# A small tile in front is widened by 128 bytes, and the tiles behind it lie elsewhere

## The chip, the cores and the metric

The kernel runs on one core of a Trainium2 chip. Its time is the device time in microseconds, the median of several runs. A profile of one execution shows what each engine did. The engines are TensorE (PE; its weight loads are listed apart, as PEld), VectorE (DVE), ScalarE (ACT), GpSimd (POOL) and SyncE (SP), which issues the DMAs here.

## What is computed

An attention with pooled keys and values, then a mixture of 8 experts with all experts weighted for each token, then a feed-forward layer with softplus. There are 2304 tokens of 512 numbers. Cut to what matters:

```
x = attention(q, k, v)                       # 4 x 8 heads, 576 queries, 72 pooled keys, width 64
P = balance(exp(x @ w_gate - max))           # 2304 x 8, rows and columns scaled 8 times
y = sum over e of P[:, e] * (relu(x @ w1[e]) @ w2[e])      # w1[e] 512 x 1024, w2[e] 1024 x 512
h = y @ w_in                                 # 512 x 2048
out = softplus(h) @ w_out                    # 2048 x 512
```

## The kernel before

Every matrix that enters one of the large products is held as two tiles, a rounded one (hi) and the rest (lo), and each product of two matrices is made of three matmuls: hi-hi, hi-lo and lo-hi. The function `three` (L439) writes them; all its matmuls have line L443 in the profile.

The work goes by units u of 512 hidden columns: 16 units for the 8 experts, 4 for the last layer (20 in all). In each unit the tokens go by 5 blocks, four of 512 and one of 256. For a block, `first_product` (L445) makes four tiles ph (f = 0 to 3) of 128 hidden columns by 512 tokens. The stationary operand (the weight that is loaded into TensorE) is a 128x128 slice of w1hi or w1lo, and the streamed operand is xhi or xlo, 512 columns at a time, 256 in the short block. ScalarE and VectorE turn ph into hhi and hlo (L469, L470); in the last four units the softplus takes eight operations and GpSimd writes hlo (L479 to L487). `second_product` (L490) then makes, for each 128 tokens of the block, a tile py of 128 tokens by 512: here a 128x128 slice of hhi or hlo is the stationary operand, the weight that is loaded, and w2hi or w2lo is streamed. There are 18 such tiles to a unit and 12 matmuls to a tile. The "second product's weight tiles" of this case are therefore hhi and hlo.

The order of the instructions is the order of the code: the first product of a block runs ahead by two tiles f (SKEW), then the second product of the block before follows. In the first unit the attention's steps stand between the products. In the units of the experts, the gate (`gate`, L317, tiles pg, stationary wg_r of 16 columns, streamed x) and the balancing are put between the products, and later a conversion of the last layer's weights.

Tiles get their place in memory by pools, one after the other from the left: const, xT (xhi, xlo), w (w1hi, w1lo, w2hi, w2lo), raw, sk, and behind them what is opened later (first the pools h0, ld, at and ld_x, then h, tmp and dec in the same place). The bytes for each of the 128 partitions, and where they lie:

```
start 16512; ident 512, ones 512, wg 128, wg_r 256   -> wg_r at 17664 = 34 x 512 + 256
xhi, xlo 36864 each                                  -> xhi at 17920 = 35 x 512, xlo at 54784 = 107 x 512
12 tiles w1hi .. w2lo, 2 raw tiles, 4096 each        -> w1hi at 91648 = 179 x 512, w2hi at 116224 = 227 x 512
prob 576, row 96 (72 and padding), col 64, big 32, lg 1152
pools h0 (later h): hhi, hlo 2048 each               -> the first at 150912 = 294 x 512 + 384
```

A slice for one matmul is 512 bytes further than the slice before it (128 numbers of 4 bytes), so all slices of hhi and hlo start 384 bytes past a multiple of 512, and all of w1hi, w1lo, w2hi, w2lo, xhi and xlo at one. (wg_r's four slices start 64 bytes apart.) Tiles in pools opened on the right side (acc0, acc1, ld_e, at_e) are placed from the other end.

Of the kernel before, what the change touches and what calls it, by code (L numbers as in the profile page):

```python
# [9 lines left out]
F32 = mybir.dt.float32  # L10
# [9 lines left out]
def attention_moe_softplus_kernel(  # L20
# [15 lines left out]
    E = w_gate.shape[1]  # L36
# [10 lines left out]
    P = 128  # L47
# [23 lines left out]
    kpool = ctx.enter_context(tc.tile_pool(name="sk", bufs=1))  # L71
# [12 lines left out]
    prob = kpool.tile([P, NT, E], F32, name="prob")  # L84
    row = kpool.tile([P, NT], F32, name="row")

    col = kpool.tile([P, 2 * E], F32, name="col")[:, :E]
    big = kpool.tile([P, 2], F32, name="big")
    lg = kpool.tile([P, NT, 2 * E], F32, name="lg")
    nc.scalar.preload_act_table_set("natural_log_exp_and_others")  # L90
# [526 lines left out]
```

## Time and profile before

| what | before |
|---|---|
| median of 3 runs | 2134.09 us (2132.28 to 2134.9) |
| profiled execution, its own time | 2131.61 us |
| its span, first to last instruction | 2129.8 us |
| mean granted TensorE clock | 0.997 |
| TensorE busy | 2108.9 us (99%) |
| VectorE, ScalarE, GpSimd busy | 975.7, 534.8, 409.4 us |

The span is what the profile's rows cover; the profiled execution's own time is 1.8 us more, and the runs of the table's first line lie a little higher still. A granted clock of 1.00 is the 2.4 GHz level of TensorE's two (1.2 and 2.4 GHz). "The chain that ended last" follows the work back from the last instruction to whatever released each step.

### The profile page before, as it was taken

The numbers are of one execution on the slowest core, as the hardware profiler recorded it, in microseconds if no ns is written. First come the engines' busy times: TensorE is split into PE (matmuls) and PEld (weight loads), VectorE is DVE, ScalarE is ACT, GpSimd is POOL, SyncE is SP. The second block draws the span as 40 slices with busy tenths as digits, with TensorE's granted clock in tenths as the row PEclk, the third lists the DMA queues.
The fourth block names the chain that finished last, engine by engine and source line by source line (L and its number), as shares of the span: only waits on it lengthen the run. The fifth ranks groups of instructions, "written<-read, shape, count | busy, mean of one in ns | idle before, by whom it ended". The sixth has DMA issues, their size and how long they took to land.

```text
span 2129.8 us, 24079 instructions
## 1 busy us (share of the span) xinstructions
PE 2108.9 (99%) x9893; PEld 1727.8 (81%) x9893; DVE 975.7 (46%) x1574; ACT 534.8 (25%) x946; POOL 409.4 (19%) x281
## 2 busy tenths in 40 slices
PE   7999999999999999999999999999999999999999
PEld 5777788888888888888888888888888878888887
DVE  7772344544334433444344344222222355667665
ACT  4443211111111111111111111111111246545443
POOL 5441101111110101111101111110101023333332
PEclk8999999999999999999999999999999999999999
DMA  6320101111111101111111111000100000000001
GB/s 167 100 72 12 38 11 55 40 45 50 50 36 49 60 25 60 40 45 50 59 40 45 40 60 35 25 30 10 30 10 30 11 30 11 30 11 30 11 35 54
DMA packets 66333, 87.54 MB, mean 41 GB/s; under 512 B 22448, under 2 KB 38832, under 8 KB 66224
## 3 DMA queue, kind: packets, MB, share of 16 engines
q1 hardware_dynamic: 66224, 86.01, 13.0%
q8 instruction: 77, 1.26, 0.2%
q14 instruction: 32, 0.26, 0.0%
HBM read 72.89 MB, written 13.11 MB: 40 GB/s over the span
## 4 chain that ended last, share of the span: by engine, by line
PE 94%; DVE 3%; ACT 1%; POOL 1%; issue 0%; DMA 0%; SPq 0%; POOLq 0%; ACTq 0%; DVEq 0%
PE py L443 46%; PE ph L443 44%; PE px L249 1%; PE s L209 1%; DVE cr L483 1%; PE pa L238 1%; POOL hlo L487 1%; PE pg L317 0%; PE pt L516 0%; DVE ln L485 0%; DMA qt<-in_q_dram 0%; PE pq L181 0%; ACT ex L480 0%; ACT ln L482 0%; ACT cr L481 0%
## 5 line engine op out<-in xcount | busy, mean ns | idle before, releaser
L443 PE MATMUL ph<-xhi,w1hi 128*128 128x512 f32 (+1 forms) x1600 | 591.7, 370 | 0.0
L443 PE MATMUL ph<-xhi,w1lo 128*128 128x512 f32 (+1 forms) x1600 | 589.4, 368 | 0.0
L443 PE MATMUL ph<-xlo,w1hi 128*128 128x512 f32 (+1 forms) x1600 | 589.1, 368 | 0.0
L443 PE MATMUL py<-w2hi,hhi 128*128 128x512 f32 x1440 | 571.4, 397 | 0.0
L443 PE MATMUL py<-w2hi,hlo 128*128 128x512 f32 x1440 | 569.0, 395 | 0.8 <-POOL hlo L487 0.2
L443 PE MATMUL py<-w2lo,hhi 128*128 128x512 f32 x1440 | 567.9, 394 | 0.0
L469 ACT ACTIVATE hhi<-ph 128x512 fp32r<-128x512 f32 (+1 forms) x320 | 177.9, 556 | 1191.1 <-PE ph L443 1149.2
L470 DVE SCALAR_TENSOR_TENSOR hlo<-ph,hhi 128x512 fp32r<-128x512 f32 (+1 forms) x320 | 203.8, 637 | 541.0 <-ACT hhi L469 540.9
L507 DVE SCALAR_TENSOR_TENSOR acc<-py,prob,acc 128x512 f32<-128x512 f32 x252 | 189.1, 751 | 386.9 <-PE py L443 386.4
L443 PEld LDWEIGHTS ph<-xhi,w1hi 128*128 128x128 f32 x1600 | 301.6, 189 | 55.5 <-issue 3.9
L443 PEld LDWEIGHTS ph<-xlo,w1hi 128*128 128x128 f32 x1600 | 301.6, 189 | 51.1 <-DVE xlo L252 0.6
L443 PEld LDWEIGHTS ph<-xhi,w1lo 128*128 128x128 f32 x1600 | 301.6, 188 | 50.6
L443 PEld LDWEIGHTS py<-w2hi,hlo 128*128 128x128 f32 x1440 | 271.1, 188 | 68.0 <-POOL hlo L487 4.7
L443 PEld LDWEIGHTS py<-w2hi,hhi 128*128 128x128 f32 x1440 | 271.3, 188 | 65.9 <-issue 5.0
L443 PEld LDWEIGHTS py<-w2lo,hhi 128*128 128x128 f32 x1440 | 271.5, 189 | 61.1
L121 POOL TENSOR_TENSOR w1lo<-w1raw,w1hi 128x1024 fp32r<-128x1024 f32 x40 | 98.0, 2450 | 457.1 <-ACT w1hi L120 457.1
L121 POOL TENSOR_TENSOR w2lo<-w2raw,w2hi 128x1024 fp32r<-128x1024 f32 x40 | 97.2, 2431 | 397.9 <-ACT w2hi L120 397.8
L487 POOL TENSOR_TENSOR hlo<-ln,hhi 128x512 fp32r<-128x512 f32 (+1 forms) x80 | 104.9, 1311 | 271.1 <-DVE hhi L486 223.7
L421 POOL TENSOR_TENSOR dt<-dt,da 128x512 f32<-128x512 f32 x32 | 41.4, 1295 | 493.6 <-issue 297.6
L483 DVE SCALAR_TENSOR_TENSOR cr<-cr,ex 128x512 f32<-128x512 f32 (+1 forms) x80 | 75.3, 942 | 112.2 <-ACT ln L482 112.1
L479 ACT ACTIVATE ex<-ph 128x512 f32<-128x512 f32 (+1 forms) x80 | 44.2, 553 | 135.3 <-PE ph L443 132.1
L502 DVE TENSOR_TENSOR acc<-py,acc 128x512 f32<-128x512 f32 x72 | 47.5, 686 | 53.6 <-PE py L443 53.6
(86 smaller groups left out, 1107.0 us busy)
## 6 DMA issues: line engine op xcount, KB each, us to landing
w1raw<-in_moe_w_dram SPq DMA_DIRECT2D x32, 512.0 KB, 3.3
w2raw<-in_moe_w_dram SPq DMA_DIRECT2D x32, 512.0 KB, 3.5
f<-in_moe_w_in_dram SPq DMA_DIRECT2D x16, 512.0 KB, 4.2
v<-dt SPq DMA_DIRECT2D x32, 256.0 KB, 2.1
f<-in_moe_w_out_dram SPq DMA_DIRECT2D x16, 512.0 KB, 3.6
kt<-in_k_dram SPq DMA_DIRECT2D x16, 288.0 KB
qt<-in_q_dram SPq DMA_DIRECT2D x32, 144.0 KB, 2.8
vt<-in_v_dram SPq DMA_DIRECT2D x16, 288.0 KB
```

Of the source, the lines that this page charges most:

```text
L121: nc.gpsimd.tensor_tensor(lo, raw, hi.bitcast(F32), op=ALU.subtract)
L209: nc.tensor.matmul(ps[:QP, j * 2 * SP:(j + 1) * 2 * SP], qT[:, j * QP:(j + 1) * QP], kbd[g % 2])
L238: nc.tensor.transpose(pa[:SP, j * QP:(j + 1) * QP], ex[:, 2 * j + h, :], ident[:QP, :QP])
L421: nc.gpsimd.tensor_tensor(t, t, a.bitcast(F32), op=ALU.add)
L443: nc.tensor.matmul(ps, a, b, start=first and i == 0, stop=last and i == 2)
L469: nc.scalar.activation(hh, ph[:, :n], AF.Relu)
L470: nc.vector.scalar_tensor_tensor(hl, ph[:, :n], 0.0, hh.bitcast(F32), op0=ALU.max, op1=ALU.subtract)
L479: nc.scalar.activation(e, ph[:, :n], AF.Abs)
L483: nc.vector.scalar_tensor_tensor(c, c, 1.0, e, op0=ALU.subtract, op1=ALU.subtract)
L487: nc.gpsimd.tensor_tensor(hl, l, hh.bitcast(F32), op=ALU.subtract)
L502: nc.vector.tensor_tensor(a, py, a, op=ALU.add)
L507: nc.vector.scalar_tensor_tensor(a, py, prob[:, t, e:e + 1], a, op0=ALU.mult, op1=ALU.add)
```

## The change

The tile col, 8 numbers of which are used, is given 48 numbers instead of 16. That is 192 bytes instead of 64 for each partition, and all that is placed behind it from the left moves up by 128 bytes: big, lg, the tiles of the attention's pools, hhi and hlo, and the temporary tiles of the later stages. The first hhi lies at 151040 = 295 x 512 then, and all slices of hhi and hlo start at a multiple of 512. The tiles in front of col, and those placed from the right, stay where they are. Each engine has the same instructions in the same order, with the same waits.

```
-    col = kpool.tile([P, 2 * E], F32, name="col")[:, :E]
+    col = kpool.tile([P, 6 * E], F32, name="col")[:, :E]
     big = kpool.tile([P, 2], F32, name="big")
     lg = kpool.tile([P, NT, 2 * E], F32, name="lg")
```

## Rows read from the trace of the kernel before

**Rows 1.** Busy time of each engine, share of the span and instructions.

```profile
PE 2108.9 (99%) x9893; PEld 1727.8 (81%) x9893; DVE 975.7 (46%) x1574; ACT 534.8 (25%) x946; POOL 409.4 (19%) x281
```

**Rows 2.** The chain that ended last, shares by engine and by line.

```profile
PE 94%; DVE 3%; ACT 1%; POOL 1%; issue 0%; DMA 0%; SPq 0%; POOLq 0%; ACTq 0%; DVEq 0%
PE py L443 46%; PE ph L443 44%; PE px L249 1%; PE s L209 1%; DVE cr L483 1%; PE pa L238 1%; POOL hlo L487 1%; PE pg L317 0%; PE pt L516 0%; DVE ln L485 0%; DMA qt<-in_q_dram 0%; PE pq L181 0%; ACT ex L480 0%; ACT ln L482 0%; ACT cr L481 0%
```

**Rows 3.** Pieces of that chain, 724 to 791 us: start, length, what, count.

```profile
724.84 10.90 PE ph L443 x48
735.74 11.16 PE py L443 x48
746.89 10.89 PE ph L443 x48
757.78 11.15 PE py L443 x48
...
779.83 11.16 PE py L443 x48
```

**Rows 4.** Two of its longest pieces in the whole span.

```profile
790.99 11.20 PE ph L443 x72
...
2109.26 16.75 PE py L443 x72
```

**Rows 5.** Busy time, granted clock and DMA in three of those pieces.

```profile
core 0: us, PE busy (x) PEld busy (x) DVE busy (x) ACT busy (x) POOL busy (x), PEclk, DMA share, GB/s
735.74:746.89 11.15, 11.15 (x49) 9.04 (x49) 2.94 (x4) 0.60 (x1) 3.47 (x2) 1.00 0.34 118
746.89:757.78 10.89, 10.89 (x50) 9.01 (x49) 4.19 (x7) 2.73 (x4) 1.07 (x1) 1.00 0.00 0
757.78:768.93 11.15, 11.15 (x50) 9.04 (x49) 5.60 (x9) 0.60 (x1) 2.12 (x2) 1.00 0.13 48
```

**Rows 6.** Timeline of TensorE around a gate: start, length, operation, count.

```profile
209.76 1.09 PE L317 MATMUL pg<-xhi,wg_r 128*16 128x512 f32 x4
210.69 1.09 PE L317 MATMUL pg<-xlo,wg_r 128*16 128x512 f32 x4
211.62 0.40 PE L443 MATMUL ph<-xhi,w1hi 128*128 128x512 f32 x1
```

**Rows 7.** Groups of matmuls and weight loads by form: busy us, mean ns.

```profile
L443 PE MATMUL py<-w2hi,hhi 128*128 128x512 f32 x1440 | 571.4, 397 | 0.0
L443 PE MATMUL py<-w2hi,hlo 128*128 128x512 f32 x1440 | 569.0, 395 | 0.8 <-POOL hlo L487 0.2
L443 PE MATMUL py<-w2lo,hhi 128*128 128x512 f32 x1440 | 567.9, 394 | 0.0
...
L443 PEld LDWEIGHTS ph<-xhi,w1hi 128*128 128x128 f32 x1600 | 301.6, 189 | 55.5 <-issue 3.9 <-PE px L249 0.4 <-DVE mx L216 0.4
...
L443 PEld LDWEIGHTS py<-w2hi,hhi 128*128 128x128 f32 x1440 | 271.3, 188 | 65.9 <-issue 5.0 <-PE px L249 0.4
```

**Rows 8.** Pieces of the chain in the softplus stage.

```profile
2065.17 1.59 POOL hlo L487
2066.77 0.04 issue
2066.81 8.87 PE py L443 x37
```

**Rows 9.** Waits of the weight loads: us in total, times, longest us.

```profile
PEld py L443 <- POOL hlo L487: 4.7, 9, 0.6
```

**Rows 10.** Groups on VectorE and ScalarE by form: busy us, mean ns.

```profile
L470 DVE SCALAR_TENSOR_TENSOR hlo<-ph,hhi 128x512 fp32r<-128x512 f32 x256 | 176.9, 691 | 490.4 <-ACT hhi L469 490.4
L519 DVE TENSOR_TENSOR xlo<-pt,xhi 128x512 fp32r<-128x512 f32 x18 | 12.4, 689 | 4.6 <-ACT xhi L518 4.6
...
L469 ACT ACTIVATE hhi<-ph 128x512 fp32r<-128x512 f32 x256 | 153.3, 599 | 1140.8 <-PE ph L443 1102.8 <-DVE db L413 21.2 <-DVE dt L416 10.6
L518 ACT CAST xhi<-pt 128x512 fp32r<-128x512 f32 x18 | 10.5, 584 | 48.1 <-PE pt L516 48.1
```

## The prediction, made before the changed kernel was run

> **What bounds the kernel now.** I read the busy table first. TensorE is busy 99% of the span and VectorE, the next, 46% [rows 1]. A busy share does not prove a bound, so the chain that ended last comes next: 94% of it is TensorE, and two lines hold nearly all of that, the second product (py, 46%) and the first product (ph, 44%) [rows 2]. So what changes is the time from the start of one matmul to the start of the next, and nothing else has much weight. I call that time the pitch. The duration of a single matmul is no use for it, since matmuls overlap.
>
> The pitch is read from the pieces of the chain, each of which is an unbroken run of matmuls. In the middle of the program 48 first-product matmuls take 10.89 or 10.90 us and 48 second-product matmuls 11.15 or 11.16 us [rows 3]: 226.9 ns against 232.5 ns, though both stream 512 columns of 4-byte numbers through a 128x128 weight. The reader is to see these 5.6 ns (2.4%): they are the whole subject. In a longer piece the short block's matmuls of 256 columns stand: 24 x 226.9 ns and 48 of the short ones make 11.20 us [rows 4], so a short one takes 119.9 ns. The 256 columns more cost 107.0 ns, 0.418 ns each, one column per cycle at the 2.4 GHz level (granted clock 1.00 in these stretches [rows 5]). So a first-product matmul is 213.9 ns of columns and 13 ns of something that does not depend on the width; a second-product matmul is 213.9 + 18.6 ns.
>
> Is the second product slower because of what the other engines do beside it? Two runs of it with 34% and 13% of DMA, 2.94 and 5.60 us of VectorE, take the same 11.15 us, and a first-product run with more VectorE than the former takes 10.89 [rows 5]. At the very end of the program the same pitch returns: 72 in 16.75 us, 232.6 ns [rows 4]. So the loss belongs to TensorE's own two reads. The weight loads have records of the same length in both products, 188 to 189 ns [rows 7], and are shorter than the pitch; the loss does not show there as a longer load.
>
> What differs between the two products? Order (hi-hi, hi-lo, lo-hi) and shapes are the same. The streamed tiles xhi, xlo, w2hi and w2lo all start at multiples of 512 bytes, and so do the first product's weights (slices of w1hi and w1lo). Only hhi and hlo, the second product's weights, start 384 bytes past such a multiple. There is one more witness: the gate matmuls, whose stationary wg_r lies at 256, 320, 384 and 448 bytes past a multiple and which stream the very same x as the first product. Eight of them go from 209.76 to 211.62 us [rows 6], 232.5 ns each. So the streamed x is not what makes the first product quick; the weight's place (or, for the gate alone, its width of 16 columns) is.
>
> **The change part by part.** It removes, adds and reorders no instruction. It adds 128 bytes in front of everything that stands behind col in memory.
>
> *The second product.* There are 3 x 1440 = 4320 of its matmuls [rows 7], each with a weight load. After the change they read weights at multiples of 512 and stream from multiples of 512, as the first product does with weights and streams at many different such multiples. I take the first product's pitch for them: 4320 x (11.16 - 10.89)/48 us = 4320 x 5.6 ns = 24.3 us. The bounds of this unknown: nothing (no row shows hhi at another place), and up to 4320 x 18.6 ns = 80 us if all that is not columns went away; no run of the first product comes near that, and I take its value, the nearest row, since shape, order and alignment would then be the same.
>
> *The edges between products.* The pieces of 10.89 us include the change-over from and to the second product. If a little of the loss sits there too, it goes as well: 95 runs of the first product (19 units, 5 blocks) by 0.01 us (10.89 against 10.90, the resolution of the rows) is about 1 us more gain at most.
>
> *What is late next.* In the last four units (the softplus stage) the second product has to wait for hlo: GpSimd works on it for 1.59 us, and TensorE goes on with the remaining 37 of 48 matmuls 0.04 us after its end [rows 8]. There are 9 such waits [rows 9]. Their chain starts at a first-product matmul, whose time is unchanged, and 11 second-product matmuls cover it; they become 11 x 5.6 = 62 ns shorter, so the wait grows by as much: 9 x 0.06 = 0.6 us given back. If every second-product matmul of that stage (864) gave its gain back, it would be 4.8 us. In the first unit, where attention's work stands between the products, 216 matmuls gain 1.2 us, and I count half of it as lost in waits: 0.6 us.
>
> *Other tiles that move.* The attention's tiles go from one mixture of places to another (keys kp, values vp and one of two qT from multiples of 512 to 128 past; half the raw q from 384 to 0). Their matmuls are few: the lines of s, pa, pq and px hold about 3% of the chain together [rows 2], and a loss of 2.4% on all of them would be 1.5 us. Both signs are open; I take 0. VectorE and ScalarE write hlo and hhi at another place. Off multiples of 512 these take 691 and 599 ns; the same operations into xlo and xhi, which lie at multiples, take 689 and 584 [rows 10]. They are hidden under TensorE except in the waits just counted, so: nothing.
>
> *Sum.* -24.3 - 0.5 (edges, the middle) + 0.6 + 0.6 = -23.6, rounded to -24 us. The profiled execution has a span of 2129.8 us and its own time of 2131.6, so 1.8 us lie around the span; the new span would be about 2106 and that execution's time 2108. The median of the runs shown, 2134.1, lies 2.5 us above the profiled one, so I forecast 2134.1 - 24 = 2110 us.
>
> **The rivals.**
>
> *The place does not matter: same, 2134 us.* Then the second product's 5.6 ns come from something that I do not see, such as the tiles' distance in memory or how soon they were written, and all pitches stay. For it: no row shows hhi at another place, and the load records are equally long [rows 7]. Against it: the gate, whose weights were written long before and lie elsewhere, has the slow pitch too [rows 6]. The Trainium skill would decide for this rival: "SBUF — State Buffer", section "Who interferes with whom", says that TensorE has two independent read ports, one for the streamed operand and one for weight loads, and never waits on anyone, and "TensorE: Matmul & The Clock Gate", section "Step-by-step: what each phase is for", that loading the next weights takes no read bandwidth from the running matmul. By these no start address costs time and the sum is 0. The trace does not bear them out here: the two products with equal shapes differ by 5.6 ns. Chance 0.11.
>
> *Only a part is had: about 2122 us.* If 512 bytes is not the whole condition, the pitch falls to somewhere between 226.9 and 232.5 ns; half of 24 us gives 2122. Against it: the first product keeps its pitch over runs that use different multiples. Chance 0.06.
>
> *Slower: 2166 us.* Equal places could make the load and the stream meet more often. The first product has one step of 13 ns over its columns; the second has 18.6/13 = 1.43 steps on average. If aligned h met the stream twice for each matmul, the pitch would be 213.9 + 26 = 239.9 ns and the program 4320 x 7.4 ns = 32 us longer. It decides from an average above 1.43 steps. For it: both operands would then start alike, and equal starts are where a clash would be expected. Against it: the first product has equal starts and one step. Chance 0.05.
>
> **How the numbers follow.** The forecast has the remaining 0.78. Its own range: all edges gained, nothing given back and the lowest of the runs shown (1.8 us under the median) give 2134.1 - 25.3 - 1.8 = 2107, and with 1.5 us from the attention's tiles and the rounding, 2104; the softplus stage giving back all its 4.8 us, the first unit its 1.2 and the attention 1.5 leaves 24.3 - 7.5 = 16.8, so 2117. The range asked for adds the lower part of the partial case and some room for a waiting stage that I sized too small: 2104 to 2126. About 0.2% (4 us) is what a measurement of this kernel can tell from no change. Faster holds the forecast and the partial case, 0.84; same 0.11; slower 0.05.
>
> **What would show it.** Right: chain pieces of 48 py at 10.88 to 10.90 us, ph unchanged, load records still 188 ns, the gate still at 232 ns (wg_r does not move), the hlo waits longer by some 0.06 us each, the order of the lines by chain share unchanged, with py at about 45%. Wrong at the first step: py pieces still at 11.16 us. Wrong in size: another value than 10.89, which then says how many steps of 13 ns are left. What would make the forecast wrong though the pitch falls: waits in the softplus stage of more than 1 us together beyond those of before, or a first unit whose time does not move.

## The result and the profile after

The changed kernel takes 2112.55 us, the median of 5 runs (2110.2 to 2113.75), against 2132.77 us (5 runs, 2132.02 to 2134.9): a ratio of 0.9902, 95% interval 0.9888 to 0.9916. That is 20 us less; forecast were 24 us less and a time of 2110 us. The profiled execution has a span of 2110.8 us, 19.0 less than before.

The pieces of the chain that ended last show where it came from. Start in us, length in us, what, count, as in [rows 3]:

```profile
721.26 10.88 PE ph L443 x48
732.14 10.88 PE py L443 x48
...
786.54 11.19 PE ph L443 x72
797.73 10.91 PE py L443 x48
```

The second product, 11.15 to 11.16 us before, now takes what the first takes: 226.7 ns from one matmul to the next in both. The first product lost its last 0.01 to 0.02 us for each run too. The piece of 10.91 us stands behind the short block: its first five matmuls start 228 to 236 ns apart, the others 226 or 227 (from the starts in the trace).

The page's busy line and the groups by form (busy us, mean ns), which answer to [rows 1, 7, 10], cut:

```profile
PE 2088.0 (99%) x9893; PEld 1726.4 (82%) x9893; DVE 976.6 (46%) x1574; ACT 534.6 (25%) x946; POOL 408.0 (19%) x281
```

```profile
L443 PE MATMUL py<-w2hi,hhi 128*128 128x512 f32 x1440 | 564.0, 392 | 0.0
...
L443 PEld LDWEIGHTS py<-w2hi,hhi 128*128 128x128 f32 x1440 | 270.4, 188 | 60.1 <-issue 4.8 <-PE px L249 0.4
...
L470 DVE SCALAR_TENSOR_TENSOR hlo<-ph,hhi 128x512 fp32r<-128x512 f32 x256 | 176.8, 691 | 492.1 <-ACT hhi L469 492.1
L469 ACT ACTIVATE hhi<-ph 128x512 fp32r<-128x512 f32 x256 | 153.0, 598 | 1127.1 <-PE ph L443 1095.2 <-DVE db L413 21.2 <-DVE dt L416 10.6
```

TensorE is busy 21 us less and all else is as it was. The load's own record is 188 ns long as before, the writes into hhi and hlo are no faster. Whoever looks for the loss in the durations of loads finds nothing, before and after. The mean duration of the second product's matmuls did fall, from 397 to 392 ns.

Two things went against the change, and they are in two other views. The first is the clock. Busy time and granted clock in four stretches of the first 70 us (columns as in [rows 5], TensorE alone), the kernel before and then the changed one (cut):

```profile
core 0: us, PE busy (x), PEclk, DMA share, GB/s
28.00:35.00 7.00, 6.98 (x33) 0.52 0.77 201
42.00:49.00 7.00, 5.88 (x27) 0.52 0.29 99
51.00:55.00 4.00, 4.00 (x28) 1.00 0.01 4
61.00:68.00 7.00, 7.00 (x43) 1.00 0.45 103
```

```profile
42.00:49.00 7.00, 4.55 (x34) 1.00 0.41 106
...
61.00:68.00 7.00, 7.00 (x20) 0.51 0.16 48
```

In both kernels the clock is granted at half (the 1.2 GHz level) in stretches of about 7 us early on. Before, the second lies at 42 to 49 us, among attention steps in which TensorE waits for others anyway. In the changed kernel's profiled execution it lies at 61 to 68 us, on an unbroken run of first-product matmuls: 20 matmuls in the stretch, not 43. From 50 to 60 us, at a granted clock of 1.00, TensorE was busy 8.68 us. The low stretch costs 3.1 us, read between two steps of attention with the same work between them, first in the kernel before (4.96 us from start to start), then in the changed one (8.06 us):

```profile
60.18 0.69 PE L238 MATMUL pa<-ident,ex 96*72 96x96 f32 x6 [0.63 <-POOL ex L227]
...
65.14 0.41 PE L181 MATMUL pq<-ident,qt 96*128 96x96 f32 x3
```

```profile
60.22 0.69 PE L238 MATMUL pa<-ident,ex 96*72 96x96 f32 x6 [0.63 <-POOL ex L227]
...
68.28 0.41 PE L181 MATMUL pq<-ident,qt 96*128 96x96 f32 x3
```

The two kernels stand level at 60.2 us, so the low stretch of the kernel before at 42 to 49 us cost it nothing by then. The first gate starts at 212.39 us, 2.6 us later than before [rows 6], so the first unit gained 0.5 us behind the low stretch:

```profile
212.39 1.09 PE L317 MATMUL pg<-xhi,wg_r 128*16 128x512 f32 x4
```

The second is the wait for hlo in the softplus stage (weight loads' waits: us in total, times, longest us): 6.0 us where it was 4.7 [rows 9].

```profile
PEld py L443 <- POOL hlo L487: 6.0, 10, 0.7
```

The nine waits in the last three units have 5.3 us where they had 4.7. The tenth is new; it has 0.7 us and stands at 1749 us, behind the change to the last layer.

### The profile page after: what moved, and what is told of

Its sections match the earlier page's. It is cut to its first block, busy times and chain, and to the rows that moved or that the text cites. A ratio compares the mean times of both kernels' runs of the same rounds, so it can differ in the third digit from the quotient of the medians.

```text
span 2110.8 us, 24079 instructions
## 1 busy us (share of the span) xinstructions
PE 2088.0 (99%) x9893; PEld 1726.4 (82%) x9893; DVE 976.6 (46%) x1574; ACT 534.6 (25%) x946; POOL 408.0 (19%) x281
## 4 chain that ended last, share of the span: by engine, by line
PE 93%; DVE 4%; ACT 1%; POOL 1%; issue 0%; DMA 0%; SPq 0%; POOLq 0%; ACTq 0%; DVEq 0%
PE py L443 45%; PE ph L443 44%; PE px L249 1%; PE s L209 1%; DVE cr L483 1%; POOL hlo L487 1%; PE pa L238 1%; PE pg L317 0%; DVE ln L485 0%; PE pt L516 0%; ACT cr L481 0%; ACT ln L482 0%; ACT ex L480 0%; DVE ln L484 0%; PE pq L181 0%
## 5 line engine op out<-in xcount | busy, mean ns | idle before, releaser
L443 PE MATMUL py<-w2hi,hhi 128*128 128x512 f32 x1440 | 564.0, 392 | 0.0
L443 PE MATMUL py<-w2hi,hlo 128*128 128x512 f32 x1440 | 561.5, 390 | 1.8 <-POOL hlo L487 1.5
L443 PE MATMUL py<-w2lo,hhi 128*128 128x512 f32 x1440 | 561.0, 390 | 0.0
```

What stands on the lines that cost most here:

```text
L443: nc.tensor.matmul(ps, a, b, start=first and i == 0, stop=last and i == 2)
```

## The experiments

Theory A: the start of the weight that is loaded, against the start of the operand that is streamed, sets the pitch. It has two forms. A1: only the difference of the two starts counts. A2: the loaded weight must itself lie at a multiple of 512. Rival B: the place is not the cause at all, but something else that moved with it. Each edit is made to the changed kernel. Where a run needed room, one of the three buffers of vp was given up or row, col and big were put into lg, which is dead by then; that touches the first unit and the balancing only. The pieces of the chain are read in the expert units, away from both. Each experiment was run once, and its time has the clock's 3 us in it or not, so the verdicts rest on the pieces.

**h_at_128**

```
-    col = kpool.tile([P, 6 * E], F32, name="col")[:, :E]
+    col = kpool.tile([P, 10 * E], F32, name="col")[:, :E]
```

> hhi and hlo start 128 bytes past a multiple of 512 (col wider by another 128 bytes; one of three buffers of vp given up to make room, which may change waits in the first unit). Theory A, the start within 512 bytes of the weight that is loaded, against that of the streamed operand, sets the pitch: 48 second-product matmuls take more than the 10.88 us of the changed kernel, up to about 11.2, and the time is 2115 to 2140 us. Theory B, it was not the start but something else that the change did (distance to other tiles, another waiting engine): 10.88 us again and about 2112 us.

2131.2 us. The chain's pieces:

```profile
724.76 10.90 PE ph L443 x48
735.66 11.16 PE py L443 x48
```

The whole gain is undone by moving the tiles 128 bytes further in the same direction. B falls: more distance to the other tiles is not what helped.

**h_at_256** (col of 14 * E)

> hhi and hlo 256 bytes past a multiple of 512, one vp buffer fewer. Theory A: slow again, 48 matmuls in 11.0 to 11.2 us, the gate (whose weight lies at 256 and more) at 232 ns being the nearest witness. Theory C, what counts is 256 bytes and not 512: 10.88 us as at a multiple of 512, about 2112 us.

2110.4 us, and

```profile
740.73 10.88 PE ph L443 x48
751.61 10.88 PE py L443 x48
```

Theory C held and my reading of theory A, with 512 bytes as the condition, did not: 256 bytes past a multiple of 512 is as good as the multiple.

**both_at_384**

```
         lo = wpool.tile(list(raw.shape), F32R, tag=f"w{kind}lo", name=f"w{kind}lo")
+        if (kind, u, h) == (1, 0, 0):
+            wpool.tile([P, 96], F32, name="pad2", bufs=1)
```

> w2hi and w2lo (streamed) and hhi and hlo (loaded) all start 384 bytes past a multiple of 512; one vp buffer fewer. Theory A1, only the distance between the two starts counts (0 here): 48 second-product matmuls in 10.88 us, about 2112 us. Theory A2, the loaded weight's own start counts: 11.15 us, about 2133 us.

2111.5 us. hhi and hlo lie 384 bytes past a multiple here, exactly as in the kernel before, and the second product is fast:

```profile
731.42 10.89 PE py L445 x48
742.32 10.89 PE ph L445 x48
```

So it is not the weight's own place. A1 stands, A2 falls.

Where the products change, x at a multiple of 512 is streamed while hhi at 384 is loaded, or the reverse. There the starts in the trace have a last step of 233 ns and a first one of 231, and 227 between them: that is the 0.01 us over 10.88.

**stream_at_320** (the same pad of 320 bytes, with h at multiples of 512)

> hhi and hlo at multiples of 512, the streamed w2hi and w2lo 320 bytes past one (row, col and big put into the dead lg to make room). Theory A1, only the distance counts: slow, 48 second-product matmuls in 11.0 to 11.2 us, 2120 to 2135 us. Theory A2, the loaded weight's own start counts: 10.88 us, about 2112 us.

2127.0 us; hhi and hlo are at the changed kernel's good places, and the second product is slow because its stream was moved:

```profile
746.29 10.93 PE ph L444 x48
757.22 11.00 PE py L444 x48
```

Less slow than at 128 bytes, though, and the first product behind it loses 0.05 us at the change-over.

**w1_at_128** (w1's pool moved behind w2's, and a pad of 128 bytes in front of it)

```
+    w2pool = ctx.enter_context(tc.tile_pool(name="w2", bufs=3))
     wpool = ctx.enter_context(tc.tile_pool(name="w", bufs=3))
...
-    col = kpool.tile([P, 6 * E], F32, name="col")[:, :E]
+    col = kpool.tile([P, 2 * E], F32, name="col")[:, :E]
...
+    wpool.tile([P, 32], F32, name="pad1", bufs=1)
```

> The first product is given the second's fault: w1hi and w1lo start 128 bytes past a multiple of 512 over streamed x at a multiple, while hhi and hlo and w2hi and w2lo lie at multiples (w1 and w2 change their order in memory). Theory A1 (the distance between load and stream within 256 bytes sets the pitch, whatever the tile): 48 first-product matmuls in 11.15 us instead of 10.88, second-product ones 10.88; 3840 x 5.6 ns = 21.5 us on the changed kernel's 2112.5, so about 2134, a few us more if the matmuls of 256 columns lose as well. Theory D, the loss belongs to hhi and hlo (written shortly before they are loaded): 10.88 us for both, 2112 us.

2129.3 us. The roles are exchanged:

```profile
735.55 10.89 PE py L446 x48
746.44 11.16 PE ph L446 x48
757.60 10.89 PE py L446 x48
768.49 11.16 PE ph L446 x48
```

The first product's weights are written in the unit before, and they lose the same 0.27 us for 48. Rival D, that the loss belongs to freshly written h, falls. The span is 2127.5 us, 19.3 above that of the changed kernel's second profile (changed_again, below) and not 21.5 or more: the matmuls of 256 columns did not lose, they gained about 1 ns each (960 of them, 1 us). The rest of the difference lies outside the expert units: twelve of those are 13.5 us longer than in changed_again, 1.13 us each, about what the two pitches give.

**lo_at_384**

```
             hh = hpool.tile([P, 512], F32R, tag="hhi", name="hhi")
+            if (u, b, f) in ((0, 0, 0), (1, 0, 0)):
+                hpool.tile([P, 96], F32, name="pad", bufs=1)
```

> hhi at multiples of 512, hlo 384 bytes past one, one vp buffer fewer. Each third weight load of the second product is then off. If a load pays only for itself: a third of 5.6 ns on average, 48 matmuls in 10.97 us, about 2120 us. If a load that is off disturbs the ones that follow it (at the changes between the products of the kernel before the first 1 to 3 matmuls were slow): 11.05 to 11.16 us, 2126 to 2134 us.

2125.9 us and

```profile
756.56 11.09 PE py L443 x48
```

A third of the loads off costs (11.09 - 10.88)/(11.16 - 10.88) = 75% of the loss, so it is not a price for each load alone. The starts in the trace show where it falls (means of some 900 steps of each kind, 330 to 1580 us): 226.8 ns from the hi-hi to the hi-lo matmul, 232.5 ns from there to the one that loaded hlo, 234.1 ns from that to the next hi-hi, whose weight hhi starts at a multiple of 512. The load that is off slows the step in front of its matmul and the step behind it.

**gate_at_512** (the gate's weights copied into a temporary tile, each slice of 16 columns at a multiple of 512)

```
-    wg_r = cpool.tile([P, KC, 2 * E], F32R, name="wg_r")
+    cpool.tile([P, KC, 2 * E], F32R, name="wg_old")
+    wg_r = tpool.tile([P, KC, P], F32R, tag="cr", name="wg_r")[:, :, :2 * E]
```

> All else as in the changed kernel, but the gate's four weight slices of 16 columns lie each at a multiple of 512 (in a temporary tile that is free at that time) and stream x from multiples. Theory A1 says that equal starts give the first product's pitch: 8 gate matmuls in 1.81 us. If the gate's pitch comes from its width of 16 columns: 1.86 us again. The total hardly changes: 32 matmuls by 5 ns are 0.2 us.

The eight matmuls go from 207.95 to 209.81 us, 1.86 us as before [rows 6]:

```profile
207.95 1.09 PE L315 MATMUL pg<-xhi,wg_r 128*16 128x512 f32 x4
208.88 1.09 PE L315 MATMUL pg<-xlo,wg_r 128*16 128x512 f32 x4
209.81 0.39 PE L441 MATMUL ph<-xhi,w1hi 128*128 128x512 f32 x1
```

Equal starts did not help the gate, so its pitch was no witness for the place. The run's span, 2107.3 us (time 2109.1), is 3.5 us below the changed kernel's profiled one, for two other reasons. The first is its stretch at 61 to 68 us:

```profile
61.00:68.00 7.00, 7.00 (x41) 1.00 0.51 136
```

The clock was whole there, 41 matmuls ran and not 20. The second is the edit itself. It takes the cast of the gate's weights out of the first unit, where the changed kernel has it on VectorE:

```profile
51.80 3.01 DVE L295 CAST wg_r<-wg 128x32 fp32r<-128x32 f32 x1
```

Without it VectorE and the attention steps that hang on it are 1.3 us ahead at 60 us. About 0.9 us of these gains is lost again at the change to the last layer, where this run has two waits for hlo and the changed kernel one.

**h_at_64** and **h_at_32** (col of 8 * E and 7 * E)

> hhi and hlo 64 bytes past a multiple of 512, streams at multiples. Theory A1 in steps of 128 bytes: the loss grows with the distance up to 128 bytes and is about half at 64, 48 matmuls in 11.0 us, as where the stream lay 320 bytes off (distance 64 the other way), 2122 to 2128 us. If any distance but 0 and 256 costs all: 11.16 us, 2134 us. A lower pitch than 10.88 us would show a place that is better than equal starts.

> hhi and hlo 32 bytes past a multiple of 512 over streams at multiples. If the loss grows evenly from 0 bytes (226.7 ns) to 64 (233.3 ns): about 230 ns, 48 matmuls in 11.04 us, about 2126 us. If any start that is not equal costs all: 233 ns, 11.2 us, 2139 us. Below 10.88 us it would be a better place than equal starts.

2139.4 and 2137.8 us. The piece of each:

```profile
761.81 11.20 PE py L443 x48
```

```profile
738.92 11.20 PE py L443 x48
```

Neither grows evenly with the distance: 32 bytes off already cost all, and both are slower than the kernel before.

**h_at_480** (col of 5 * E)

> hhi and hlo 480 bytes past a multiple of 512, 32 bytes in front of the streams' place within 256. If the loss grows evenly to the 229 ns seen at 64 bytes in front (stream at 320, h at 0): about 228 ns, 48 matmuls in 10.94 us, about 2118 us. If the load in front of the stream by less than a step costs nothing: 10.88 us. Below it: a better place than equal starts.

2138.9 us. The loss is the same 32 bytes in front as 32 bytes behind, and the estimate of a mild loss was wrong:

```profile
739.85 11.19 PE py L443 x48
```

**h_at_192** (col of 12 * E)

> hhi and hlo 192 bytes past a multiple of 512 over streams at multiples; one vp buffer fewer. The distance within 256 bytes is that of the run with streams at 320 and h at 0. Theory A1 (only the distance counts): the same pitch as there, 229.2 ns, 48 matmuls in 11.00 us, about 2122 us. If the places themselves count as well: another pitch, 232 to 233 ns as at the other unequal starts, 2134 to 2139 us.

2119.4 us and

```profile
734.36 10.99 PE py L443 x48
745.35 10.88 PE ph L443 x48
```

As in stream_at_320 (11.00), where the difference of the starts is the same within 256 bytes and both places are others. A1 once more. The pieces of 48 by that difference:

```
load minus stream, bytes mod 256     0       32     64     128         192           224
48 second-product matmuls, us   10.88-10.89  11.20  11.20  11.15-11.16 10.99-11.00   11.19
```

**changed_again** (no edit)

> The changed kernel once more, for the place of the stretches of 1.2 GHz in the first 80 us. Matmul pieces as before, 10.88 us for 48. If the second such stretch falls at 61 us again, on dense first-product matmuls: span about 2110.8. If it falls elsewhere or is not there: 2106 to 2109, as in the kernel with the gate's slices at multiples of 512 (2107.3).

Span 2108.2 us, 2.6 below the first profile of the same program. The clock's second low stretch lay elsewhere and was shorter:

```profile
51.00:55.00 4.00, 4.00 (x14) 0.57 0.00 0
61.00:68.00 7.00, 6.94 (x47) 1.00 0.34 93
```

This stretch halves the matmuls too (14, not 27), but attention steps behind it wait in any case: this run is 0.55 us behind the first profile at 49 us and 0.60 us behind it at 61 us.

## Why the prediction was right, and where it was not

*The pitch.* Right, and the largest term: the second product took the first product's pitch. It was sized from a piece of 10.89 us, which held a little of the loss at its edges; with 10.88 the term is 4320 x 0.28/48 = 25.2 us and not 24.3, and the edges that were listed apart came as well. The bound of 80 us was never near: 13 ns over the columns remain at equal starts.

*The condition.* Wrong in its form. The prediction took multiples of 512 bytes as what the operands must share. The runs show that only the difference between the two starts counts, within 256 bytes: weights at 384 over a stream at 384 are fast, 256 over 0 is fast, 0 over 320 is slow. For this change both rules give the same time, so it was luck that the forecast did not suffer.

*The gate as a witness.* This step failed. The gate's slow pitch was held against the rival that the place does not matter; with equal starts the gate keeps its 232.5 ns, so it says nothing on places (whether that is its 16 columns was not tried apart). What the prediction had left against that rival was the two products with equal shapes, and that was enough, as w1_at_128 shows from the other side.

*Other engines beside it.* Right: the pitch is the same beside much or little work of the others, and it moves with the places alone. That VectorE and ScalarE would not be faster was right too, though the rows compared other operations (ACTIVATE with CAST, SCALAR_TENSOR_TENSOR with TENSOR_TENSOR [rows 10]).

*The Trainium skill's rival.* "SBUF — State Buffer", section "Who interferes with whom", has TensorE with two independent read ports and never waiting on anyone. No run here bears it out that place costs nothing, for a stream of 512 columns beside a load of 128: 48 matmuls take from 10.88 to 11.20 us by the two starts alone. The measurement decides.

*What is late next.* Too small. The nine waits for hlo grew by 0.6 us, as sized, but the tenth adds 0.7, and together they pass the 1 us that the prediction itself had named as a sign of trouble. There was also no term for the slow first matmuls behind each interruption. At the change to the last layer eight pieces of 12 second-product matmuls stand between transposes (L516); they took 2.78 to 2.80 us and take 2.78, where 12 x 226.7 ns would be 2.72.

*The slower rival.* It said that equal starts are where load and stream would clash. The opposite holds: equal starts are the best of the six distances, and small differences cost more than the kernel before ever lost.

*The missing 4.6 us of the profiled span (19.0 against 23.6).* The short blocks' pieces of 72 serve as marks, before and then after:

```profile
392.88 11.20 PE ph L443 x72
...
1587.20 11.20 PE ph L443 x72
```

```profile
393.50 11.19 PE ph L443 x72
...
1572.62 11.19 PE ph L443 x72
```

Twelve expert units lie between the marks; they gained 15.2 us, all that the pitch gives for their 2592 second-product matmuls. In front of the first mark stand 576 of them, worth 3.4 us, and 0.6 us were lost: 3.1 us are the clock's low stretch, for which the prediction had no term, and 0.9 us stayed in the first unit's waits (0.6 was counted). Behind the second mark stand 1152, worth 6.7 us, and 4.4 came: 2.3 us went to the waits for hlo and the slow starts, where 0.6 was counted. The low stretch is not of the change: changed_again, the same program, has none at 61 to 68 us and a span of 2108.2 us, 21.6 below the kernel before. (gate_at_512 is no clean witness, since its edit gains in the first unit.) That four of the five timed runs lie between 2112.4 and 2113.8 us, the profiled one (2112.6) among them, leaves open how often it falls so.

*The forecast time.* 2110 us lies 2.6 us from the measured 2112.55, closer than the gain (24 against 20.2), and that is luck: it was counted from 2134.1, the median of three runs, and the five have 2132.77.

*What stays open.* Why 256 bytes is the period, why 192 is milder than 64, and what the gate's 232.5 ns come from. The dependence on the difference is shown; that the two reads of TensorE hold each other up is the reading that fits it, and no view here shows a read.

## What to carry to other kernels

When two lines of equal shape have different pitches on TensorE, divide the chain's unbroken pieces by their counts; the records of the loads don't show it, and the durations of matmuls overlap. Then compare the start of each loaded weight with the start of what is streamed over it: here any difference that was tried, other than 0 modulo 256 bytes, cost 1 to 3% of the product, and a pad of 128 bytes in front of the pool set it right. Change such a pad only with the addresses of all tiles behind it in view, since a small tile that grows by 32 bytes can cost as much as 128 bytes won here (h_at_32: 2137.8 us).

## What the runs showed of the hardware

- The pitch of 512-column matmuls with 128-column loads depends on the difference of the two start addresses modulo 256 bytes: 226.7 to 226.9 ns at 0, 229.0 to 229.2 at 192, 232.3 to 233.3 at 32, 64, 128 and 224 (48 matmuls in 10.88 to 10.89, 10.99 to 11.00 and 11.15 to 11.20 us). Matmuls of 256 columns over a load 128 bytes off did not lose: a short block's piece of 24 long and 48 short ones took 11.28 us with w1 at 128 (790.53 us, below), which 24 x 232.5 ns and 48 x 118.8 make, against 119.9 before.

```profile
790.53 11.28 PE ph L446 x72
```

- The loss is no fixed price for each matmul. The steps from start to start repeat in a pattern that belongs to the difference, wherever the tiles lie and whichever product it is (medians over the pieces of 48 between 330 and 1580 us, from the starts in the traces):

```
difference  runs                          steps, ns, repeated
0           changed kernel, both_at_384   227 (both_at_384: inside the pieces)
32          h_at_32                       232 235
64          h_at_64                       231 236
128         before, h_at_128, w1_at_128   241 232 231 232 228 230 232
192         h_at_192, stream_at_320       226 229 232
224         h_at_480                      233 234 231 235
```

- One load of three off gives three quarters of the loss (lo_at_384): the step in front of its matmul and the step behind it are slow, 232.5 and 234.1 ns.
- The granted clock falls to the 1.2 GHz level for stretches of 3 to 7 us (17 us in both_at_384) in the first 70 us, at other times in two executions of one program. One of 7 us on an unbroken run of matmuls cost 3.1 us; one of 3.4 us, at 51 us in changed_again, was taken up by the waits behind it.
